# Weights of a fused attention and mixture-of-experts kernel loaded in pieces of 256 KB, with a new order of the first batch

## The chip, the cores and the metric

The kernel runs on one core of one Trainium2 chip. The metric is device time in microseconds (us), lower is better. TensorE is called PE here (its weight loads PEld), VectorE DVE, ScalarE ACT, GpSimd POOL, and SyncE, which issues every data transfer of this kernel, SP.

## The reference

There are two stages, in float32, over 8 batches, 8 heads, 576 positions and head width 64.

- Attention: `out = up(softmax(qd kd^T / 8) vd) + softmax(local(q k^T / 8)) v`. `qd`, `kd` and `vd` are means over groups of 4 positions, `up` repeats each row 4 times, and `local` keeps the positions less than 4 apart.
- The result, laid out as `x` of shape (8, 576, 512), goes through a mixture of 4 causal attention experts: `logits = x w_gate`; each expert has `q = x wq`, `k = x wk`, `v = x wv`, a causal softmax, and `(a v) wo`; for each position the two experts with the highest logits are summed, weighted by the softmax of those two logits.

## The kernel before

**Work and stages.** A batch `b` has four pairs of heads `c`. Stage 1 of a pair, written as (b, c), goes through these steps: `load` (q, k and two halves of v, with for batches from 1 on four smaller transfers of v for the pooling), `local` (scores of the band, L519, on PE), masking, maximum, exponential, sum and normalisation of them (`l_mask`, `l_max`, `l_sub`, `l_exp`, `l_sum`, `l_eps`, `l_rec`, `l_nrm`), `qd` and `kd` (means, L555 on DVE or L559 to L562 on POOL), `vd_mm` (the mean of v as a matmul, L577, in batch 0 alone), `down` (scores of the means, L594), their softmax (`d_max` to `d_nrm`), `tp` (transposes, L375, and their copies `tp_ev` out of PSUM to `pt` and `pd`, L317 or L319), `o1` and `o1d` (the matmuls with v, L656 to L668), `up`, `x`, and at last `xh` (ACT, L681), `xt` and `xl` (L684, L682), which split x into a high and a low part. Stage 2 makes the experts' `q`, `k` and `v` with three matmuls for each product (high by high, low by high, high by low; L709 and L770), and the gate. Stage 3 is the experts' causal attention (L858 to L977) and the output matmul.

**Weights.** `weights()` loads `wqk` (1 MB), `wvg` (520 KB) and `wo` (512 KB), each with one transfer into one staging tile `wst` (step `wld`). For each of the four chunks of 128 input rows (two for `wo`) ACT casts the high part (`whi`, L454), and POOL or DVE subtracts for the low part (`wlo`, L456). The staging tile of `wo` takes the place of that of `wqk`, so it waits until all chunks of `wqk` have been read.

**Order.** The program creates a list of steps, and `SEQ` says in which order they are emitted: a number divided by 4 is the step, the remainder chooses the engine where there is a choice (or which half of PSUM the `down` scores go to), and -1 is a filler matmul on zeros (L476), which also takes a PSUM buffer. Each engine works through its own queue in that order, and waits at the head of it. Four PSUM buffers `big0` to `big3` go round in the order in which they come free.

**Transfers.** Every transfer goes through `fetch` (L464) on SP's queue. From the 5th to the 60th transfer each waits for the landing of the one four places ahead, so at most four are under way (`PACE = 4, 60`). SP waits in order: what stands behind a waiting transfer waits too.

**From the start to the projections.** The first batch alone has no earlier batch beside it. PE's first projection matmul is that of `q` of batch 0; from it on PE has matmuls of several batches to choose from.

Of the kernel before, what the change touches and what calls it, by code (L numbers as in the profile page):

```python
# [277 lines left out]
def tile_attn_then_moe(ctx: ExitStack, tc: tile.TileContext, qT, kT, v, wqk, wvg, wo, out):  # L278
# [7 lines left out]
    D = 128 * NP  # L286
# [9 lines left out]
    op = plan.op  # L296

    def buf(pool, shape, name, bufs=2, dtype=F32, tag=None, fifo=True):
        b = Buf(pool, shape, dtype, name, tag or name, bufs)
        b.fifo = fifo  # L300
        return b
# [142 lines left out]
    def weights():  # L444
        for at, (src, n, m, whi, wlo) in zip(WAT, ((wqk, NP, 512, wqk_h, wqk_l), (wvg, NP, 260, wvg_h, wvg_l),
# [3 lines left out]
            st = buf(wk, [128, n, m], "wst", bufs, tag=tag)  # L449
# [678 lines left out]
```

## Time and profile before

| | |
|---|---|
| median of 3 runs | 457.27 us (454.79 to 457.93) |
| the profiled execution's own time | 455.93 us |
| its span in the trace | 454.2 us |
| instructions in the trace | 23423 |
| PE busy | 437.5 us (96% of the span) |
| DVE busy | 360.3 us (79%) |
| ACT busy | 342.9 us (76%) |
| POOL busy | 309.1 us (68%) |
| transfers, mean rate | 52.90 MB, 116 GB/s |

The span runs from the first to the last recorded instruction; the profiled execution's own time is 1.7 us more. The busy shares are averages over all stages. The page also cuts the span into 40 slices of 11.4 us, with each engine's busy share in each; the first four slices are the stage that the change touches.

### The profile page before, as it was taken

The numbers are of one execution on the slowest core, as the hardware profiler recorded it, in microseconds if no ns is written. First come the engines' busy times: TensorE is split into PE (matmuls) and PEld (weight loads), VectorE is DVE, ScalarE is ACT, GpSimd is POOL, SyncE is SP. The second block draws the span as 40 slices with busy tenths as digits, with TensorE's granted clock in tenths as the row PEclk, the third lists the DMA queues.
The fourth block names the chain that finished last, engine by engine and source line by source line (L and its number), as shares of the span: only waits on it lengthen the run. The fifth ranks groups of instructions, "written<-read, shape, count | busy, mean of one in ns | idle before, by whom it ended". The sixth has DMA issues, their size and how long they took to land.

```text
span 454.2 us, 23423 instructions
## 1 busy us (share of the span) xinstructions
PE 437.5 (96%) x9910; PEld 404.2 (89%) x9911; DVE 360.3 (79%) x1018; ACT 342.9 (76%) x1097; POOL 309.1 (68%) x507
## 2 busy tenths in 40 slices
PE   6787999999999999999999999999999999999996
PEld 4766999999998899998999998999999898999776
DVE  8778898888888699968978889678787977656862
ACT  7777689779877898776787787876797687547873
POOL 6766989996886987737886798849677464205240
PEclk9899999999999999999999999999999999999999
DMA  7665667532336552515332742256240130101022
GB/s 247 195 189 151 200 165 206 155 97 76 98 95 171 162 144 51 170 47 157 116 127 83 196 119 76 84 162 182 69 155 19 56 97 4 69 14 40 29 82 104
DMA packets 44312, 52.90 MB, mean 116 GB/s; under 512 B 4144, under 2 KB 27184, under 8 KB 44208
## 3 DMA queue, kind: packets, MB, share of 16 engines
q1 hardware_dynamic: 44208, 51.40, 38.3%
q8 instruction: 78, 1.28, 1.2%
q14 instruction: 26, 0.21, 0.1%
HBM read 40.90 MB, written 9.44 MB: 111 GB/s over the span
## 4 chain that ended last, share of the span: by engine, by line
PE 86%; DMA 7%; DVE 3%; ACT 1%; issue 1%; SPq 0%; POOL 0%; POOLq 0%
PE pj L709 23%; PE pv L709 11%; PE po L709 10%; PE sq L858 9%; PE o L968 7%; PE tq L375 5%; PE tp L375 4%; PE sc L519 4%; PE o L656 4%; PE scd L594 3%; DMA lq<-in_qT_dram 2%; DMA wst<-in_wqk_dram 2%; PE pv L770 2%; DMA lv<-in_v_dram 2%; PE o L663 2%; PE po L1007 1%
## 5 line engine op out<-in xcount | busy, mean ns | idle before, releaser
L881 ACT ACTIVATE pr<-pr,pst 128x384 f32<-128x384 f32 (+8 forms) x144 | 80.2, 559 | 18.3 <-DVE pst L878 17.3
L709 PE MATMUL pj<-xh,wqk_h 64*128 64x288 f32 x512 | 83.0, 306 | 0.0
L889 POOL TENSOR_SCALAR pr<-pr,pst,gt 128x512 f32<-128x512 f32 (+8 forms) x90 | 58.4, 657 | 31.5 <-DVE pst L886 30.0
L709 PE MATMUL pj<-xh,wqk_l 64*128 64x288 f32 x512 | 79.0, 291 | 0.0
L709 PE MATMUL pj<-xl,wqk_h 64*128 64x288 f32 x512 | 79.0, 291 | 0.0
L878 DVE CUSTOM_DVE_ANT_0 pr<-sq,causal_t 128x192 f32<-128x192 f32 (+8 forms) x144 | 64.5, 485 | 8.4 <-PE sq L858 7.8
L709 PEld LDWEIGHTS pj<-xh,wqk_h 64*128 64x128 f32 x512 | 51.7, 185 | 2.8 <-issue 1.7
L858 PE MATMUL sq<-k,q 64*64 64x64 f32 (+6 forms) x768 | 52.1, 371 | 0.0
L709 PEld LDWEIGHTS pj<-xh,wqk_l 64*128 64x128 f32 x512 | 51.6, 185 | 0.0
L709 PEld LDWEIGHTS pj<-xl,wqk_h 64*128 64x128 f32 x512 | 51.6, 184 | 0.0
L540 POOL TENSOR_TENSOR lp<-lp,lst 128x640 f32<-128x640 f32 x28 | 36.3, 1300 | 11.1 <-DVE lst L539 5.3
L858 PEld LDWEIGHTS sq<-k,q 64*64 64x64 f32 x768 | 32.2, 133 | 7.7 <-issue 0.3
L709 PE MATMUL pv<-wvg_h,xh 64*128 64x260 f32 x256 | 38.8, 292 | 0.0
L604 ACT ACTIVATE dp<-scd,dst 128x144 f32<-128x144 f32 x96 | 35.3, 376 | 4.3 <-PE sq L858 2.0
L709 PE MATMUL pv<-wvg_h,xl 64*128 64x260 f32 x256 | 37.1, 279 | 0.0
L709 PE MATMUL pv<-wvg_l,xh 64*128 64x260 f32 x256 | 37.1, 279 | 0.0
L317 ACT COPY ptb<-tq 128x384 f32<-128x384 f32 (+4 forms) x74 | 31.3, 481 | 7.2 <-PE tq L375 6.9
L709 PE MATMUL po<-oh,wo_h 64*128 64x288 f32 x224 | 35.2, 301 | 0.2
L709 PE MATMUL po<-ol,wo_h 64*128 64x288 f32 x224 | 34.5, 292 | 0.5 <-issue 0.5
L375 PE MATMUL tq<-ident,pr 64*128 64x64 f32 x736 | 33.8, 224 | 0.4 <-DVE oc L977 0.3
L709 PE MATMUL po<-oh,wo_l 64*128 64x288 f32 x224 | 34.2, 291 | 0.0
L968 PE MATMUL o<-ptb,vg 64*64 64x320 f32 (+2 forms) x512 | 31.7, 378 | 0.8 <-ACT ptb L317 0.5
(183 smaller groups left out, 1436.8 us busy)
## 6 DMA issues: line engine op xcount, KB each, us to landing
lv<-in_v_dram SPq DMA_DIRECT2D x64, 160.0 KB, 3.9
lk<-in_kT_dram SPq DMA_DIRECT2D x32, 292.0 KB, 3.9
lq<-in_qT_dram SPq DMA_DIRECT2D x32, 292.0 KB, 4.1
out_dram<-ot SPq DMA_DIRECT2D x28, 288.0 KB, 3.2
lr<-in_v_dram SPq DMA_DIRECT2D x19, 256.0 KB, 3.5
pool<-in_v_dram SPq DMA_DIRECT2D x9, 256.0 KB, 4.2
lr<-in_v_dram SPq DMA_DIRECT2D x38, 32.0 KB, 3.1
wst<-in_wqk_dram SPq DMA_DIRECT2D x1, 1024.0 KB, 8.8
```

The source lines that it names most:

```text
L317: A.copy(dst, src)
L375: T.transpose(ps()[:, 512 * x + z[x]:512 * x + z[x] + 64], data[r, 0:128], ident[r, r])
L519: T.matmul(sc()[halves[h ^ (t // 5)], 512 * (t // 5) + W * i:512 * (t // 5) + W * i + W], q()[r, z:z + 64], k()[r, z:z + W], start=True, s ...
L540: op("l_nrm", "GV", (pool_tt(n), dve(n)), lambda e: eng[e].tensor_tensor(p(), p(), st[:, :, 2:3].to_broadcast([128, NT, W]), op=OP.mult), ...
L604: A.activation(p()[:, t, :], scs()[:, at * t:at * t + SD], AF.Exp, bias=st[:, t, 4:5], scale=1.0 / 128.0, accum_out=st[:, t, 0:1])
L656: T.matmul(o()[r, 512 * x + z:512 * x + z + n], lv()[kr, t, r], pt()[kr, at, t, 0:n], start=True, stop=True)
L709: mine = T.matmul(self.out(z), self.w(c, i, z)[r], self.m(c, i, z)[r], start=phase == 0 and c == 0 and i == 0, stop=phase == 1 and c == se ...
L858: T.matmul(pss[x][0]()[halves[e ^ turned(t)], at_of[x] + at + to:at_of[x] + at + to + n1 - n0], q()[r, 64 * t:64 * t + 64], k()[r, n0:n1], ...
L878: op("s_max", "V", dve(n) + 4, lambda x=x, t=t, n=n, src=src: V.tensor_tensor_reduce(rows_of[t], src(), causal_t[:, S - 64:S + 256] if t = ...
L881: op("s_exp", "A", 281 + n / 1.2, lambda x=x, t=t, n=n: A.activation(rows_of[t], rows_of[t], AF.Exp, bias=st[:, x, 4:5], scale=-1.0, accum ...
L889: op("s_nrm", "GV", (327 + n / 1.2 + max(0, n - 384) * 1.1, 189 + n / 1.92), lambda g, x=x, t=t, n=n: eng[g].tensor_scalar(rows_of[t], row ...
L968: T.matmul(obs[x]()[r, q0:q1], vg()[kr, j, 64 * (2 * p + e):64 * (2 * p + e) + 64], pt()[kr, e, j, q0:q1], start=j == 0, stop=j == len(job ...
```

## The change

Each weight matrix is loaded in several transfers: `wqk` in four of one chunk (256 KB), `wvg` in two of two chunks (260 KB), `wo` in two of one chunk (256 KB), into the same staging tile. A chunk's cast waits for its own piece alone. That makes 5 more transfers, all through `fetch` with the same rule of four under way, so the 60th transfer comes five places earlier among the others.

The front of `SEQ` is written anew: its first 416 entries (of 2685) become 420 (of 2689). They hold the same steps, the five new transfers, and one filler matmul less. All entries behind them are the old ones with 20 added, since the five new steps shift the numbers. The new front reaches as far as the first two steps of the second half of `q` of batch 0.

```diff
@@ weights()
-            op("wld", "D", 1800 if m == 260 else 780 * n, lambda st=st, src=src: fetch(
-                st(), src.rearrange("(c p) j -> p c j", p=128)), w=[st], alloc=[st])
+            rows, step = src.rearrange("(c p) j -> p c j", p=128), 2 if m == 260 else 1
+            for c in range(0, n, step):
+                op("wld", "D", 900 if m == 260 else 780, lambda st=st, rows=rows, c=c, step=step: fetch(
+                    st()[:, c:c + step, :], rows[:, c:c + step, :]), w=[(st, c + x) for x in range(step)], alloc=[] if c else [st])
@@ SEQ (first entries; all behind entry 416 are the old ones plus 20)
-    4, 0, 177, 173, 120, 216, 136, 140, 188, 192, 268, 144, 16, -1, 197, 200, 124, 232, -1, 273, 220, 148, 236, 205,
...
```

What the new numbers mean, queue by queue:

| queue | before | after |
|---|---|---|
| SP, places 8 to 29 | k(0,3), k(1,0), q(0,3), q(1,0), v(0,1), v(0,2), v(0,1), k(1,1), q(1,2), v(0,2), **wqk**, v(0,3), v(0,3), q(1,1), **wvg**, k(1,2), k(1,3), q(1,3), then v of batch 1 | q(0,3), k(0,3), k(1,0), q(1,0), v(0,1) twice, **wqk 0**, v(0,2) twice, **wqk 1**, **wqk 2**, q(1,1), k(1,1), v(0,3) twice, k(1,2), **wvg 0**, q(1,2), **wqk 3**, **wvg 1**, k(1,3), q(1,3), then v of batch 1 |
| SP, `wo` | place 43 | place 35 (first piece) and place 49 (second) |
| SP, second half of v(1,1) | place 44 | place 47 |
| PE, ahead of the first `q` | 45 steps, 8 of them fillers | 43 steps, 6 of them fillers, the rest the same steps |
| PE, from `vd_mm`(0,0) on | vd_mm(0,0), tp(0,0), down(0,2), local(0,3), tp(0,0), o1(0,0), local(1,0), o1d(0,0), tp(0,1), vd_mm(0,1) | vd_mm(0,0), tp(0,0) twice, down(0,2), local(0,3), o1(0,0), o1d(0,0), local(1,0), tp(0,1), vd_mm(0,1) |
| PE, on to the first `q` | filler, down(0,3), tp(0,1), tp(0,2), vd_mm(0,2), o1(0,1), o1d(0,1), tp(0,2), filler, down(1,0), filler, o1(0,2), o1d(0,2), local(1,1), tp(0,3), vd_mm(0,3), 2 fillers, tp(0,3), filler, down(1,1), o1(0,3), o1d(0,3), local(1,2) | filler, tp(0,1), o1(0,1), tp(0,2) twice, o1d(0,1), down(0,3), down(1,0), filler, vd_mm(0,2), local(1,1), o1(0,2), o1d(0,2), vd_mm(0,3), tp(0,3) twice, 2 fillers, down(1,1), o1(0,3), o1d(0,3), local(1,2) |
| ACT, around the first cast of `wqk` | l_exp(0,3), xh(0,0), d_scl(0,3), tp_ev(0,1), d_exp(0,3), **whi 0**, vd_ev(0,2), l_exp(1,0), tp_ev(0,2) | l_exp(0,3), tp_ev(0,2) twice, **whi 0**, whi 2, l_exp(1,0) |
| moved from POOL to DVE, ahead of the first `q` | | qd(0,1), qd(0,2), qd(0,3), kd(0,3), wlo 2 of wqk, wlo 0, 2 and 3 of wvg |
| moved from DVE to POOL, ahead of the first `q` | | kd(0,1), kd(1,0), qd(1,0), xl and xt of (0,0), xl(0,2), wlo 3 of wqk |
| moved between ACT, POOL and DVE | d_nrm(0,0) on ACT, d_nrm(0,1) on POOL; copies of tp(0,1), vd_mm(0,3) on ACT, of tp(0,2), vd_mm(0,0) on DVE | d_nrm(0,0) on POOL, d_nrm(0,1) on ACT; the copies the other way round |

## Rows read from the trace of the kernel before

**Rows 1.** The page: busy time of each engine; PE's busy tenths in 40 slices.

```profile
PE 437.5 (96%) x9910; PEld 404.2 (89%) x9911; DVE 360.3 (79%) x1018; ACT 342.9 (76%) x1097; POOL 309.1 (68%) x507
...
PE   6787999999999999999999999999999999999996
```

**Rows 2.** Busy time by stretch (us, PE, PEld, DVE, ACT, POOL, clock, transfers).

```profile
0.00:42.09 42.09, 31.76 (x727) 25.19 (x729) 33.97 (x84) 31.90 (x106) 31.59 (x61) 0.96 0.68 197
...
45.00:400.00 355.00, 353.63 (x8280) 333.20 (x8281) 291.73 (x822) 274.32 (x885) 263.20 (x417) 1.00 0.40 116
```

**Rows 3.** Chain of work that ended last, 18 to 42 us (start, length, what).

```profile
18.75 8.79 DMA wst<-in_wqk_dram
...
27.56 0.62 ACT wqk_h L454
...
29.09 0.54 ACT pt L317
29.63 0.59 issue
...
33.51 0.46 PE tp L375 x10
...
34.83 0.65 issue
...
40.18 1.65 issue
```

**Rows 4.** Timeline of PE's weight loads: idle before and its end, in brackets.

```profile
22.05 1.08 PEld L577 LDWEIGHTS pv<-lv,pool 128*128 128x128 f32 x9 [1.25 <-issue]
...
30.22 0.10 PEld L476 LDWEIGHTS <-zero 128*128 128x128 bf16 x1 [1.50 <-issue]
...
35.48 0.63 PEld L577 LDWEIGHTS pv<-lv,pool 128*128 128x128 f32 x5 [0.84 <-issue]
...
41.83 0.19 PEld L519 LDWEIGHTS sc<-lk,lq 64*64 64x64 f32 x2 [1.78 <-issue]
```

**Rows 5.** Busy time by stretch, cut in the stops of Rows 4.

```profile
21.00:29.00 8.00, 6.66 (x126) 5.67 (x125) 6.77 (x15) 6.63 (x25) 5.35 (x7) 1.00 0.77 216
29.00:35.00 6.00, 4.46 (x126) 3.44 (x126) 4.53 (x14) 4.32 (x15) 4.43 (x6) 1.00 0.52 146
35.00:41.00 6.00, 4.65 (x126) 3.71 (x127) 5.80 (x15) 4.91 (x15) 6.00 (x7) 1.00 0.62 173
```

**Rows 6.** Transfer queues at 22.1:27.3 (all of them), 27.3:29 and 32.6:34.2 (packets, MB, share).

```profile
q1 hardware_dynamic: 1140, 1.33, 90.3%
...
q8 instruction: 1, 0.02, 5.0%
...
DMA  0009000000000000000000000000000000000000
...
q8 instruction: 1, 0.02, 5.1%
```

**Rows 7.** One tile: the fillers (ns, least, median, most).

```profile
L476 PE MATMUL wu<-zero x7: 379/389/390, 8.3 to 37.5; 128*128 128x512 bf16 x7
```

**Rows 8.** Groups by line, 4 to 42 us (busy, mean ns, idle before).

```profile
L682 POOL TENSOR_TENSOR xl<-x,xh 128x576 fp32r<-128x576 f32 x1 | 1.4, 1425 | 0.0
...
L682 DVE TENSOR_TENSOR xl<-x,xh 128x576 fp32r<-128x576 f32 x2 | 2.6, 1293 | 0.0
```

**Rows 9.** The page: transfers by line (KB each, median us to landing).

```profile
lr<-in_v_dram SPq DMA_DIRECT2D x19, 256.0 KB, 3.5
...
wst<-in_wqk_dram SPq DMA_DIRECT2D x1, 1024.0 KB, 8.8
```

**Rows 10.** Timelines: SP's places 26 and 44, and PE's first `o1` of (1,1).

```profile
36.63 0.60 SPq L464 DMA_DIRECT2D lv<-in_v_dram  x1
...
52.56 2.15 SPq L464 DMA_DIRECT2D lv<-in_v_dram  x1
...
61.55 0.30 PE L656 MATMUL o<-pt,lv 64*64 64x58 f32 x4
```

281 rows, old and new, of the table SEQ are left out of this document.

## The prediction, made before the changed kernel was run

> **What bounds the kernel now.** I read the page first. PE is busy for 96% of the span, and in the slices it is full from the fifth on; only the first four, 45 us, are at 6 to 8 tenths [rows 1]. Busy time by stretch says the same: before the first projection, which starts at 42.09, PE works 31.76 us of 42.09 and rests 10.33; from 45 to 400 it rests 1.4 us in 355 [rows 2]. Behind 45 us PE sets the pace and the order there is the old one, so what the new front can give is the time at which PE starts the projections, and it carries to the end one for one.
>
> Next the chain of waits, 18 to 42 us. It runs from the 1 MB transfer of `wqk` (18.75 to 27.54) to ACT's first cast of it at 27.56, over ACT's copy of `pt`, which ends at 29.63, to PE, and from there on it is PE itself with three stops called "issue": 0.59, 0.65, 1.65 [rows 3]. "issue" is time in which PE waits for nothing that the profile shows. The timeline of the weight loads has four such stops, ending at 22.05, 30.22, 35.48 and 41.83 [rows 4]. Counting by stretches cut in these stops shows what they are: 251, 252 and 253 matmuls and weight loads lie between one stop and the next (126 + 125, 126 + 126, 126 + 127) [rows 5]; with the few waits that PE's queue also holds, that is a block of the same number of instructions each time. The transfer queues show the other half: from 22.1 to 27.3 all packets are data, and the one packet of instructions runs in the stretch after it, in which the `wqk` transfer lands; and in 32.6 to 34.2, when the data has drained, a packet of instructions is all there is, at about 32.7 [rows 6], 2.7 us ahead of PE's restart at 35.48. So PE's instructions come in blocks, the block's packet waits behind data, and in this stage, full of short matmuls, PE gets to the end of a block before the next is there. Restart to restart takes 8.17, 5.26 and 6.35 us [rows 4]; PE's own work in those blocks is 6.66, 4.46 and 4.65 [rows 5].
>
> On this the Trainium skill ("Runtime: NRT & Kernel Launch", section Instruction fetch mechanics) says that instructions are fetched in blocks of 256 while the block before is worked on, and that crossing a boundary is mostly hidden. The count in the trace agrees with it; the stops do not. By the page the stops would have nothing to give and the result would be the second rival below.
>
> **The change, part by part.**
>
> Pieces of `wqk`. Before, the whole 1 MB had to land for ACT's first cast; the cast starts 0.02 after the landing, and it and two other steps stood ahead of the copy of `pt` [rows 3]. Now piece 0 is place 14 on SP instead of 18, it is a quarter of the size, and the cast stands behind both copies of tp(0,2). That takes ACT out of the second stop. It also takes a 1 MB transfer out of the way of the instruction packet, so I let the longest interval, 8.17, fall to what PE's work sets, 6.66 [rows 5], called 6.7; bounds 5.3 (the shortest interval) and 8.2 (nothing gained).
>
> Front of PE's queue. Ten more transposes (0.46 [rows 3]) now stand ahead of local(0,3), where PE works on the block before the first stop, so I put the first restart 0.5 later, at 22.5; bounds 0 and +0.8, the latter since qd(0,1) on DVE goes ahead of the first mask. The rest of that stretch is the same work in another order.
>
> Third and fourth block. They hold as many instructions as before. The third now has two of the mean matmuls of v in it, the fourth none, so PE's work moves from the fourth to the third, and I take the mean of the two measured intervals for each, (5.26 + 6.35) / 2 = 5.8 [rows 4]; bounds 5.3 and 6.4 each.
>
> Fillers. Two fewer stand ahead of the projections: 2 x 0.39 = 0.78 of PE work [rows 7]. It lies inside blocks that end with the refill, so 0; should the refills be quick, 0.78 is gained. One of them comes back later among busy matmuls and costs 0.39 there; I let that go into the bounds.
>
> Five more transfers. SP issues each in about 0.6 [rows 10], 3 us in all, in a stage in which it mostly waits for a slot: 0. Their landing: a transfer of 256 KB has a median of 3.5 us, the 1 MB took 8.8 [rows 9], so four in turn would be 14 and four abreast 3.5; the four pieces are spread over places 14 to 26, and chunk 3 is not needed before the fourth step of `q`, so 0, with bounds 0 and +1.
>
> Steps handed between engines. Seven means change sides, four to DVE and three to POOL; two xl go to POOL, where one takes 1.43 against 1.29 on DVE [rows 8]. Both engines are busy for 32 and 34 of the first 42 us [rows 2], so neither is full: 0. The last operand of the third step of `q`, xl(0,2), comes from POOL now; behind it there is room of some 2 us, and if that cover is gone it costs what it is late, bound +1.
>
> Sum: 22.5 + 6.7 + 5.8 + 5.8 = 40.8 for the fourth restart, and 0.26 as before from there to the first projection (41.83 to 42.09): 41.1 instead of 42.1, 1.0 us earlier. With the lower bounds 22.05 + 5.3 x 3 + 0.26 = 38.2, but the second block has 6.66 of work, so 39.5, 2.6 us earlier; with the upper ones 22.9 + 8.2 + 6.4 x 2 + 0.26 = 44.2, and 1 for the landing or for xl, which are waits of the same step, 3.1 us later. The sum is made against the profiled execution, 455.93, which gives 454.9. That execution was 1.3 under the median of the runs, 457.27; from the median it is **456.3**.
>
> **Rivals.**
>
> *No stops at all.* With small transfers the instruction packets could always be in time. Then PE needs only its work: 22.05 less the first stop of 1.25 is 20.8, and 6.66 + 4.46 + 4.65 + 0.26 make 36.8 [rows 4, 5], 5.3 earlier: 452.0. For it speaks that the packet waited behind the 1 MB. Against it: the stops at 35.48 and 41.83 came when that had long landed, with data of other transfers under way, which stay.
>
> *The change does nothing to the path.* The refills come when they came, the new order only changes which step stands at each stop: 457.3. For it: three of four stops had no part in `wqk`, and of the 1.50 of rest at the second, 0.59 is refill whatever ACT does [rows 3, 4]. Against it: the longest interval is the one with the 1 MB in it.
>
> *SP held by `wo`: slower.* The first piece of `wo` is place 35 instead of 43. It needs the staging tile, so SP stands until the last low part of `wqk` is made, now on POOL behind xl(0,2) and l_sub(1,1). Behind it wait 27 transfers of batches 1 and 2. Place 26 was issued at 36.63 and place 44 at 52.56, 0.89 each [rows 10]; the second half of v(1,1) is place 47 now, so 12 x 0.89 = 10.7 after SP is let go, and it lands 3.5 later [rows 9]. PE wanted it at 61.55 [rows 10], or 60.5 if it is 1.0 earlier. So it decides from 60.5 - 14.2 = 46.3 on, one for one: let go at 49, PE loses 2.7 and the time is 459.0. Against it: POOL's list puts that low part at about 42.
>
> The Trainium skill ("DMA: Bandwidth & Descriptors", section Bandwidth and the cost model before it) speaks against small transfers: some 2.0 us fixed for each, and 1 MiB or more in one. Five more would be 10 us in the queue, with four under way 2.5 us later, an estimate by that page; this rival would then be 461.5. Rows 9 agree in kind, 4 x 3.5 being more than 8.8.
>
> **How the numbers follow.** Forecast 456.3, chance 0.50, its own range 454.7 to 457.3 (2.6 earlier, or nothing); no effect 0.20; no stops 0.12; SP held, or the upper bounds, 0.18. The likeliest gives 456.3. A measurement of this kernel tells about 1%, 4.6 us, from no change, so the limits are 452.7 and 461.8. Faster by more than that needs nearly all stops to go: 0.11. Slower needs a hold past 52 us, or a loss behind 45 us that no row shows: 0.06. Within: 0.83. For 8 in 10 the range takes the forecast, no effect and SP held to 459.2, and on the lower side reaches from 454.7 towards the rival without stops, to 452.9.
>
> **What would show it.** Right: four stops of PE still a block apart, the second interval near 6.7 instead of 8.2, the first projection near 41, ACT's first cast without idle time before it, and from 45 us on a PE as full as before. Wrong: stops gone; intervals unchanged; PE idle in front of `o1` of (1,1) with a transfer as the releaser; or a difference that arises behind 67 us, where the order is the old one.

## The result, and the profile after

The changed kernel takes 449.80 us (median of 6 runs, 448.16 to 451.06); the kernel before, beside it, 454.97 (6 runs). The ratio is 0.988, 95% interval 0.983 to 0.992: 5.2 us or 1.2% faster. In a later series of runs it was 449.24 against 453.68, ratio 0.989 (0.984 to 0.993). The range of the prediction ended at 452.9, so the time lies outside it, next to the rival "no stops at all" (452.0). The profiled execution took 450.58, its span is 448.8.

The page after, for [rows 1]: PE works 1.7 us less in a span that is 5.4 us shorter, and is full from the third slice on instead of the fifth, but for the nineteenth (202 to 213 us).

```profile
PE 435.8 (97%) x9910; PEld 400.4 (89%) x9910; DVE 360.0 (80%) x1018; ACT 343.6 (77%) x1101; POOL 306.3 (68%) x507
...
PE   6899999999999999998999999999999999999996
```

Busy time by stretch, for [rows 2]: the first projection comes at 34.38 instead of 42.09; PE rests 5.9 us ahead of it instead of 10.3. From 45 to 400 us it rests 2.8 us instead of 1.4; 1.3 of that comes at 203 us (below).

```profile
0.00:34.38 34.38, 28.45 (x726) 22.26 (x726) 31.41 (x76) 29.16 (x96) 29.27 (x60) 1.00 0.77 227
45.00:400.00 355.00, 352.23 (x8191) 328.99 (x8191) 289.21 (x816) 273.33 (x878) 253.59 (x408) 1.00 0.39 113
```

The chain, for [rows 3]: no transfer of `wqk` in it, and from 19.22 on PE with no "issue" longer than 0.04 up to the first projection.

```profile
18.18 0.61 ACT pt L317
18.79 0.44 issue
19.22 1.72 PE pv L579 x14
...
24.95 1.83 PE pv L579 x14
...
30.27 0.99 PE tp L375 x20
...
34.45 1.40 PE pj L711 x17
```

Lines behind `weights()` have numbers 2 higher in this kernel. Of the four stops of [rows 4] one is left in the weight loads:

```profile
19.23 1.53 PEld L579 LDWEIGHTS pv<-lv,pool 128*128 128x128 f32 x13 [1.02 <-issue]
```

The stretches between the ends of the blocks (at 24.95, 30.30 and 34.38), for [rows 5]. Columns as in [rows 2]. With the waits that PE's queue holds, a block is 256 instructions, as before. PE works through all of the second stretch and nearly all of the third:

```profile
18.00:25.00 7.00, 5.81 (x131) 4.89 (x127) 6.32 (x15) 5.95 (x18) 6.07 (x9) 1.00 0.69 200
25.00:30.30 5.30, 5.30 (x126) 4.94 (x128) 5.10 (x13) 5.13 (x21) 4.74 (x5) 1.00 0.90 264
30.30:34.38 4.08, 3.92 (x131) 2.93 (x131) 3.87 (x12) 3.88 (x10) 4.08 (x5) 1.00 0.76 222
```

The transfer queues, for [rows 6], in 19.22:20.3 (data alone) and 20.3:21: the packet of instructions now starts 1.15 us behind PE's restart, where it was 5.4 before.

```profile
q1 hardware_dynamic: 134, 0.20, 54.9%
...
q8 instruction: 1, 0.02, 10.8%
```

A piece lands in 3.9 us, for [rows 9]; and SP issues the first piece of `wo` at 36.96, so it is not held, and the second half of v(1,1) at 48.36 instead of 52.56, for [rows 10].

```profile
wst<-in_wqk_dram SPq DMA_DIRECT2D x4, 256.0 KB, 3.9
```

```profile
36.96 0.55 SPq L466 DMA_DIRECT2D wst<-in_wo_dram  x1
...
48.36 0.60 SPq L466 DMA_DIRECT2D lv<-in_v_dram  x1
```

### The profile page after: what moved, and what is told of

Read it like the earlier page. It is cut to its first block, busy times and chain, and to the rows that moved or that the text cites. A ratio compares the mean times of both kernels' runs of the same rounds, so it can differ in the third digit from the quotient of the medians.

```text
span 448.8 us, 23428 instructions
## 1 busy us (share of the span) xinstructions
PE 435.8 (97%) x9910; PEld 400.4 (89%) x9910; DVE 360.0 (80%) x1018; ACT 343.6 (77%) x1101; POOL 306.3 (68%) x507
## 3 DMA queue, kind: packets, MB, share of 16 engines
q8 instruction: 78, 1.28, 1.3%
## 4 chain that ended last, share of the span: by engine, by line
PE 88%; DMA 3%; DVE 3%; ACT 3%; issue 1%; POOL 1%; SPq 1%; DVEq 0%; POOLq 0%
PE pj L711 22%; PE pv L711 10%; PE po L711 9%; PE sq L860 9%; PE o L970 8%; PE tq L375 5%; PE tp L375 4%; PE o L658 4%; PE sc L521 4%; PE scd L596 3%; PE o L665 2%; DMA lr<-in_v_dram 2%; PE pv L772 2%; PE po L1009 1%; PE pv L579 1%; PE o L974 1%
## 5 line engine op out<-in xcount | busy, mean ns | idle before, releaser
L711 PE MATMUL pj<-xh,wqk_h 64*128 64x288 f32 x512 | 81.6, 306 | 0.0
L711 PE MATMUL pj<-xl,wqk_h 64*128 64x288 f32 x512 | 78.1, 291 | 0.0
L711 PEld LDWEIGHTS pj<-xh,wqk_h 64*128 64x128 f32 x512 | 50.5, 185 | 2.0 <-issue 1.0
L711 PEld LDWEIGHTS pj<-xh,wqk_l 64*128 64x128 f32 x512 | 50.4, 185 | 0.8 <-issue 0.8
L711 PEld LDWEIGHTS pj<-xl,wqk_h 64*128 64x128 f32 x512 | 50.4, 184 | 0.2 <-issue 0.2
L711 PE MATMUL po<-oh,wo_l 64*128 64x288 f32 x224 | 34.2, 291 | 0.0
L375 PEld LDWEIGHTS tq<-ident,pr 64*128 64x128 f32 x736 | 30.0, 138 | 3.8 <-issue 2.3
```

Of the source, the lines that this page charges most:

```text
L375: T.transpose(ps()[:, 512 * x + z[x]:512 * x + z[x] + 64], data[r, 0:128], ident[r, r])
L711: mine = T.matmul(self.out(z), self.w(c, i, z)[r], self.m(c, i, z)[r], start=phase == 0 and c == 0 and i == 0, stop=phase == 1 and c == se ...
```

## The experiments

In all of them "stop" is a rest of PE at the end of a block, and "packet" the start of PE's packet of instructions, found by narrowing the stretch in the view of the queues. "Behind" counts from PE's restart at the end of the second block, unless a crossing (PE's passing from one block into the next) is named. The expectations count blocks from the kernel's start: there the second block ends near 19 us (22 where its stop is long), and the third to fifth are those that the prediction calls the second to fourth.

**Either half alone.** The pieces with the old order, and the new order with whole matrices.

```diff
 split_only: weights() and pieces of the kernel after; SEQ of the kernel before,
+            the extra pieces right behind the first of their matrix
 order_only: weights() of the kernel before; SEQ of the kernel after,
-            without the extra pieces
```

> The order of the kernel before, with the three weight matrices in pieces of 256 KB; the extra pieces stand right behind the first piece of their matrix on SP, everything else is in its old place. Theory T (transfers): PE's instruction packets wait behind data in the transfer engines, and smaller pieces let them through. Then the four refill stops, 4.84 us in sum before, fall to about 1.5 us, the packet at 27.4 comes near 24, the first projection comes near 38.5 instead of 42.1, and the time is about 3 us (0.7%) below before. Theory O (order): the gain comes from the new order of the first batch. Then the stops stay between 4 and 5 us in sum, the first projection stays at 41 to 42, and the time is within 0.2% of before.

> The new order of the first batch, with each weight matrix in one transfer again, at the place of its first piece. Theory T: the first operand of the v mean still lands about 1 us earlier, and PE works there at full clock, together 2.3 us; but the refill stops come back (3 us or more in sum) where wqk is under way, so the first projection comes near 38.5 to 40 and the time is 2 to 3 us below before. Theory O: the first projection comes at 34.5 to 35 as in the kernel after, with at most one stop, and the time is within 0.2% of the kernel after (5 us below before).

Neither half gives anything by itself: 453.52, ratio 0.999 (0.996 to 1.001), and 454.34, ratio 1.003 (1.000 to 1.006). The weight loads of the first show three stops (that at the end of the third block is gone):

```profile
19.31 1.42 PEld L586 LDWEIGHTS pv<-lv,pool 128*128 128x128 f32 x12 [1.15 <-issue]
...
32.13 0.97 PEld L586 LDWEIGHTS pv<-lv,pool 128*128 128x128 f32 x8 [1.66 <-issue]
...
38.59 0.19 PEld L528 LDWEIGHTS sc<-lk,lq 64*64 64x64 f32 x2 [1.89 <-issue]
```

and those of the second a single one, three times as long:

```profile
21.89 2.85 PEld L584 LDWEIGHTS pv<-lv,pool 128*128 128x128 f32 x13 [3.34 <-issue]
```

Its packet starts at 19.28, 4.0 us behind PE's crossing into the block before (15.32), with the 1 MB under way; with pieces it was 1.05 (15.20 to 16.24), and 0.7 to 2.7 in the five profiles with that front. Behind that stop the granted clock falls, which is one more loss, and eleven of the twelve runs have a mean clock of 0.988 to 0.996 as the profiled one has (0.996), so the long stop is hardly that execution's alone. The same kernel's PE by stretch (busy, clock, transfers):

```profile
20.00:25.00 5.00, 3.11 (x15) 0.66 0.76 185
```

Neither theory was right. The order takes away the stops at the ends of the third to fifth block, but with the 1 MB whole the one at the end of the second grows to 3.45. The pieces shorten that one in the new order; in the old order they do not (1.07, against 1.17 and 0.66 in two profiles with whole matrices). It needs both.

**Depth of the transfers.**

```diff
-PACE = 4, 60
+PACE = 8, 60        (after_pace8; before_pace2 has 2 in the kernel before)
```

> The kernel after, with eight transfers under way at a time instead of four in the first sixty. Theory T: packets wait behind twice as much data; they start 2 to 4 us past the block's boundary instead of 0.9 to 1.3, two or three stops of 0.6 to 1.5 us come back, and the first projection moves from 34.4 to 36 or 37. Theory O: the depth of the data queue is nothing to PE; the first projection stays within 0.5 us of 34.4, or comes earlier because loads land earlier.

> The kernel before, with two transfers under way at a time instead of four in the first sixty. Theory T: where the queue holds less data the packets come sooner, so the stops at 35.5 and 41.8 shrink below 0.3 us each, while the one behind the 1 MB of wqk stays; PE waits longer for loads instead, so the time can go either way. Theory O: the stops stay at their four places with 4 to 5 us in sum, and later loads only add waits: first projection later than 42.1 and the time above before.

With eight under way the packets start 3.9 us behind the crossing at 14.96 and 4.1 behind the restart at 21.79; one stop of 3.71 comes of it, the first projection is at 38.53, and the time 452.01, ratio 0.996 (0.993 to 0.999). So the packet came later with more data under way, though there was one long stop, not the two or three expected. With two under way PE waits for loads (2.81 and 4.13 us and more), 479.25, ratio 1.056; a packet came 7.2 us behind its crossing even there, and three stops stayed (1.91, 0.29 and 0.55), so that run did not tell the theories apart.

**The same kernels once more.**

> The kernel before, unchanged, profiled once more, to see what in its first 42 us is the kernel's and what is that one execution's. Theory C (a chain of late blocks: a block of PE instructions that comes late is followed by late ones until PE has long work): four stops at the same four places again, 4 to 5.5 us in sum, packets 2.3 to 5.4 us behind the crossings, PE going on 2.4 to 2.9 us behind each packet. The late landing at 12.81 and the low clock behind it are that execution's: here the first v mean starts near 11 at full clock, and the first projection comes near 40. Rival: landing and clock are the kernel's as well, and the first projection comes at 42 again.

> The kernel after, unchanged, profiled once more. Theory C: the stop at the end of the second block is about 1 us at most, no other stop ahead of the first projection, which comes at 34 to 35; the losses at 203 us (1.4) and 260 us (0.7) are that execution's and are not there again, or stand elsewhere. Rival: they belong to the kernel, since everything is earlier by 7 us there, and come again within 1 us of the same places.

The kernel before (453.63) has its first v mean at 10.39 and its first projection at 38.06, 4.0 us earlier than in the execution on which the prediction was built. The four stops are there again (3.81 us in PE's idle time, 4.84 in the first profile):

```profile
18.54 1.42 PEld L577 LDWEIGHTS pv<-lv,pool 128*128 128x128 f32 x12 [0.74 <-issue]
...
26.16 0.10 PEld L476 LDWEIGHTS <-zero 128*128 128x128 bf16 x1 [0.95 <-issue]
31.45 0.97 PEld L577 LDWEIGHTS pv<-lv,pool 128*128 128x128 f32 x8 [0.80 <-issue]
37.80 0.19 PEld L519 LDWEIGHTS sc<-lk,lq 64*64 64x64 f32 x2 [1.78 <-issue]
```

with PE's own work in the three blocks as in [rows 5], and a low clock behind the last stop, which costs 1.4 us: the 127 matmuls of 37.80:45.00 take 7.20, and as many take 5.77 behind the same stop in the first profile (41.83:47.60), where the clock is 1.00:

```profile
18.00:26.00 8.00, 6.66 (x126) 5.67 (x125) 7.28 (x15) 5.89 (x23) 4.89 (x7) 1.00 0.89 240
26.00:31.40 5.40, 4.45 (x126) 3.45 (x126) 4.41 (x13) 5.34 (x17) 5.40 (x6) 1.00 0.66 194
31.40:37.80 6.40, 4.65 (x127) 3.71 (x128) 6.13 (x15) 5.26 (x18) 6.40 (x8) 1.00 0.54 151
37.80:45.00 7.20, 7.20 (x127) 6.71 (x128) 4.57 (x7) 2.76 (x6) 3.48 (x6) 0.76 0.71 192
```

The kernel after (446.81) has one stop of 0.33, its first projection at 33.51, and lost nothing at 203 or 260 us. So the two losses were not in every execution; that at 203 us came again in a third profile (below).

**Which matrix, and three under way.**

```diff
 wqk_pieces: weights(), new SEQ without the second pieces of wvg and wo
-  rows, step = ..., 2 if m == 260 else 1
+  rows, step = ..., 1 if (n, m) == (NP, 512) and whi is wqk_h else n
 after_pace3: PACE = 3, 60 in the kernel after
```

> The new order, with wqk alone in pieces; wvg and wo go in one transfer each, at the place of their first piece. Theory C: what decides is that the packet for the third block, requested at about 15 us, gets past wqk; so the stop there stays near 1 us, no other one follows, the first projection stays at 34 to 35.5, and the time is within 0.3% of the kernel after, 1% below before. Rival (any transfer over 256 KB holds a packet up): wvg, 520 KB at about 25 us, delays the packet behind 24.95, a stop of 1 us or more comes at 30.3, and half of the gain is gone.

> The kernel after, with three transfers under way at a time instead of four in the first sixty. Theory C: less data ahead of the packets, so no refill stop is left; but two transfers under way already gave a kernel whose PE waits for loads, so waits for q, k and v of 0.5 to 2 us each come in their place, and the time is 0 to 2% above the kernel after. Rival (the data is what holds PE up in the whole stage): without any stop the first projection comes at 33.5 or earlier, and the time falls by another 0.2%.

`wqk` alone in pieces gives the whole gain: 449.57, ratio 0.985 (0.979 to 0.991), first projection 34.50, one stop of 0.95; the 520 KB of `wvg` did no harm. With three under way PE rests 0.56 at the end of the second block, where a load of v comes last, but it waits 1.92 and 2.12 us for k and q of batch 1: 454.82, ratio 1.003 (0.999 to 1.006).

**Whose order.** The new front could be split between SP and the four other engines (not between PE and the other three, whose orders hang together).

```diff
 sp_new: weights() in pieces; SP's steps in the order of after, all other engines' as before
 sp_old: weights() in pieces; SP's steps in the old order, all other engines' as after
```

> The loads on SP in the new order, with pieces; PE, DVE, ACT and POOL in the old order (SP's list of the kernel after, everything else from the one before). Theory S: what lies in the transfer engines when PE asks for a block decides, so SP's order is the half of the new order that counts: packets 0.4 to 2 us behind the crossings, no stops at the ends of the third to fifth block, the first projection at 35 to 36, and the time 4 us (0.9%) below before. Theory P: PE's own order decides (where its long and its short work lies between the crossings): packets 2.3 us or more behind the crossings, two or three stops of 0.6 to 1.7 us as in the split kernel with the old order, the first projection at 38 to 39, and the time within 0.4% of before.

> The reverse: the loads on SP in the old order, the extra pieces right behind the first of their matrix, and PE, DVE, ACT and POOL in the new order. Theory S: stops of 0.6 to 1.7 us at the ends of the third to fifth block, the first projection at 38 to 39, the time within 0.4% of before. Theory P: after the end of the second block no stop, packets 0.4 to 2 us behind the crossings, the first projection at 34 to 36, and the time 3 to 5 us below before; a wait for a load that the new order wants earlier could cost up to 1 us of it.

SP's new order alone: 454.84, ratio 0.999 (0.996 to 1.002). Its profile is better than that, with two stops and the first projection at 36.59:

```profile
18.62 1.42 PEld L586 LDWEIGHTS pv<-lv,pool 128*128 128x128 f32 x12 [0.60 <-issue]
...
36.33 0.19 PEld L528 LDWEIGHTS sc<-lk,lq 64*64 64x64 f32 x2 [0.90 <-issue]
```

but it was one of four runs at 451.2 to 452.3, all with a mean clock of 1.00; the other eight took 454.4 to 455.4, seven of them at 0.989 to 0.996. The other engines' new order with the old loads: 451.42, ratio 0.992 (0.989 to 0.995), with one stop and none behind it, although PE waited 1.82 us for a k at 6 us in its profile, whose execution, 454.44, was slower than all its others but one:

```profile
21.16 2.83 PEld L586 LDWEIGHTS pv<-lv,pool 128*128 128x128 f32 x13 [1.60 <-issue]
```

So theory P holds for the larger part. And the packet goes with PE's order, not with what SP has under way: 3.4 us behind in sp_new, 1.1 in sp_old. The expectation "2.3 or more" in sp_new was right there and two blocks on (4.2), and wrong in between (1.2).

**Where the block begins, or what lies in it.**

```diff
-WAT, NW0 = (53.0, 30.0, 67.0), 7
+WAT, NW0 = (53.0, 30.0, 67.0), 8     (split_nw8, on split_only; after_nw6 has 6 in the kernel after)
```

> The old order with pieces, and one more matmul of zeros ahead of everything (eight instead of seven), which moves every block boundary of PE two instructions back in the work: the third block then begins with the first instruction of a group of v means, as in the new order, instead of inside it. Theory P1 (where the boundary falls in PE's stream decides how soon the next packet comes): the packet behind that boundary starts 1.1 to 1.6 us behind PE's restart instead of 3.4 to 5.4, one or two of the later stops go, and the first projection comes at 35.5 to 37.5. Theory P2 (what work lies between the boundaries decides): packets 3 us or more behind, stops at the ends of the fourth and fifth block again, the first projection at 38 to 39, the time as that of the split kernel with the old order.

> The kernel after with one matmul of zeros less ahead of everything (six instead of seven), which moves every block boundary two instructions on: the third block begins inside the group of v means, as in the old order. Theory P1: the packet behind that boundary starts 3 us or more behind the restart, stops of 0.6 us or more come at the ends of the third to fifth block, the first projection moves to 36.5 to 38, and half of the gain is gone. Theory P2: the packet starts 1.1 to 1.6 us behind the restart, there is no stop behind the second block, and the first projection stays at 33.5 to 36.5 and the time within 0.3% of the kernel after.

P2 holds on both sides. In the old order the packet is 5.0 us behind and PE rests at the same four block ends (0.78, 0.54, 1.31 and 1.48; the first of them ends with ACT's copy of `pt`, 3.4 us behind its packet), first projection 38.59, 452.91, ratio 0.997 (0.993 to 1.000). In the new order it is 1.9 behind, there is no stop at all, first projection 33.55, 448.31, ratio 0.988 (0.982 to 0.994), which can't be told from the kernel after.

**The loss at 203 us, and a faster version.**

```diff
 SP, from place 145:  load of pool for (4,2), half of v (4,2),
+  both loads of lr for (4,3),
   load of pool for (5,1) (held until 194 us), lr for (5,0), half of v (4,3),
-  both loads of lr for (4,3),
```

> The kernel after, with the two loads of lr for (4,3) moved on SP from place 150 to right behind place 146, ahead of the transfer for which SP is held until 194; they are issued near 190 instead of 196. In three of five profiles with the new order the landing of this lr at about 199.7 lets POOL start its 1.9 us xl ahead of DVE's vd, which then takes 1.54 instead of 0.53, and PE loses 1.3. If this is what gives back part of the gain, DVE waits for nothing there, vd takes 0.53 in the profile, PE has no idle time at 200 to 205, and the median falls by 0.5 to 1 us below that of the kernel after (to about 1.3% below before). Rival: DVE waits there for something else as well or PE has the slack, and the time stays within 0.2% of the kernel after.

> The kernel after, unchanged, timed next to the same kernel with lr earlier, since the two were only compared over different calls. The median lies at 448.5 to 450, the ratio to before at 0.986 to 0.990; in its profile the first projection at 33.5 to 36.5 by the stop at the end of the second block (0.3 to 2.3 us).

> The kernel after with the two loads of lr for (4,3) earlier on SP, unchanged, next to the kernel after. If DVE's wait for that lr costs PE 1.3 us in three of five executions, the median is 0.5 to 1 us below that of the kernel after of this call. Rival: the difference seen before was one of chips and calls, and the two medians lie within 0.4 us.

447.82, ratio 0.985 (0.982 to 0.989); and beside the kernel after in one series 447.31 against 449.24 (ratios to before 0.985 (0.980 to 0.989) and 0.989 (0.984 to 0.993)): 1.9 us, more than the 0.5 to 1 expected; the fastest version here. In the third profile of the kernel after DVE waits for `lr`, POOL starts `xl` ahead of DVE's `vd`, and PE loses 1.13. DVE, POOL and PE there:

```profile
201.19 0.74 DVE L573 TENSOR_TENSOR lr<-lr 128x512 f32<-128x512 f32 x1 [1.25 <-DMA lr<-in_v_dram]
201.97 1.53 DVE L574 TENSOR_TENSOR vd<-lr 128x256 f32<-128x256 f32 x1
...
201.35 1.87 POOL L684 TENSOR_TENSOR xl<-x,xh 128x576 fp32r<-128x576 f32 x1
...
204.94 0.40 PE L375 MATMUL tq<-ident,pr 64*128 64x64 f32 x6 [1.13 <-DVE pd L319]
```

With `lr` earlier (second profile) there is no wait, `vd` runs ahead of `xl`, and PE has no idle time at 200 to 205:

```profile
198.25 0.67 DVE L580 TENSOR_TENSOR lr<-lr 128x512 f32<-128x512 f32 x1
198.96 0.48 DVE L581 TENSOR_TENSOR vd<-lr 128x256 f32<-128x256 f32 x1
...
200.42 1.43 POOL L691 TENSOR_TENSOR xl<-x,xh 128x576 fp32r<-128x576 f32 x1
```

Two of three profiles of the kernel after have this loss, neither of the two with `lr` earlier. What gives the rest of the 1.9 us was not looked for.

Up to some 190 us the kernel with `lr` earlier is the kernel after, so its two profiles are two more of the new front. The first of them has the longest stop of the five, and its first projection at 36.35; its time, 450.49, and that of one more run, 450.13, lie above the other four (447.27 to 447.86). PE there, its stop and the stretch around the restart (busy, clock, transfers):

```profile
21.19 1.72 PE L586 MATMUL pv<-lv,pool 128*128 128x128 f32 x14 [2.29 <-ACT lp L539]
...
20.00:25.00 5.00, 3.81 (x85) 1.00 0.75 212
```

The packet starts at 18.52, 2.7 us behind the crossing at 15.83, with pieces and four transfers under way; PE goes on 2.7 behind it. So the length of the first stop differs from one execution to the next even in the changed kernel.

## Why the prediction was wrong, step by step

PE's idle time at block ends ahead of the first projection, its start, and the packet behind the restart, from the profiles:

| kernel | stops, us | first projection | packet behind |
|---|---|---|---|
| before; once more | 4.84; 3.81 | 42.09; 38.06 | 5.4; 4.8 |
| before, two under way | 2.75 | 48.58 | 7.2 (crossing) |
| old order, pieces | 4.29 | 38.84 | 3.8 |
| old order, pieces, blocks moved | 4.11 | 38.59 | 5.0 |
| SP new, others old, pieces | 1.28 | 36.59 | 3.4 |
| SP old, others new, pieces | 1.71 | 37.94 | 1.1 |
| new order, whole matrices | 3.45 | 38.47 | 2.0 |
| after, eight under way | 3.71 | 38.53 | 4.1 |
| after, three profiles | 1.13; 0.33; 1.18 | 34.38; 33.51; 34.63 | 1.2; 1.6; 2.5 |
| after, `lr` earlier, two profiles | 2.29; 0.35 | 36.35; 33.62 | 1.1; 2.1 |
| after, `wqk` alone in pieces | 0.95 | 34.50 | 1.1 |
| after, three under way | 0.56 | 35.88 | 1.1 |
| after, blocks moved | 0 | 33.55 | 1.9 |

**What was right.** PE sets the pace behind 45 us and a gain at the first projection reaches the end; the stops are block ends (256 instructions apart, 251 to 254 of them matmuls and weight loads and the rest waits of PE's queue; where nothing else comes last, PE goes on 2.2 to 3.0 us behind a packet). The five transfers and the handed steps, put at 0, cost nothing: from 19.22 to the first projection PE waits for no transfer and no other engine. SP was let go at 36.96, ahead of the 46.3 from which the rival with `wo` would have decided. The first restart was to come 0.5 later: 18.54 in the repeated kernel before, 18.35, 18.46, 18.89, 19.22 and 21.19 in the five profiles of the new front, a median of 0.35 later.

**The step that failed** is "third and fourth block": it let the stops stay, at the mean of the measured intervals, 5.8 each, with bounds 5.3 and 6.4. After the change (in the prediction's count) the third takes 5.36 and the fourth 4.07 (24.95, 30.31, 34.38), which is PE's own work in them; the second takes 5.73 where 6.7 was put, since the new order has other work in it. Together 15.2 instead of 18.3. The stop at the end of the fourth was back once, with 0.52 in the third profile. The two fillers, put at 0 "should the refills be quick, 0.78", then counted.

**The argument that misled** was "the stops at 35.48 and 41.83 came when that had long landed, with data of other transfers under way, which stay". It is true that they don't hang on `wqk`: the new order with whole matrices has none there either. But they don't hang on that data: they go with the order of PE and the three engines beside it, which the prediction treated as "the same work in another order". That every packet waits behind data does not hold in the kernel before itself. Between PE's restart at 35.48 and the packet at 39.13 the transfer engines stood empty for 1.1 us; their busy tenths in 35.5:39, 40 slices:

```profile
DMA  9952000000000000000699593955789877879999
```

The repeated profile shows the same (empty from 31.96 to 33.20, packet at 35.04). The 0.12 for "no stops at all" was far too low, and the range stopped short of it.

**The base** was an execution with 4.0 us of its own ahead of the first projection: the v mean waited for v until 12.81, and the granted clock was 0.79 in 10:15 and 0.87 in 15:20 (1.00 in both after). In 20 of 29 runs of the kernel before in one series, and 10 of 23 in another, the mean clock was 0.999 or more, so that part is not in every execution. The median of three runs that the forecast started from, 457.27, was also 2.3 above that of the six (454.97), so of the 6.5 us between 456.3 and 449.80 some 2.3 are the base and 4.2 the gain, 5.2 instead of 1.0. The base did not spoil the sum, which was a difference, but the rival's 36.8 came from it; by the repeated profile it would have been 17.8 + 6.66 + 4.45 + 4.65 + 0.26 = 33.8, and 33.5 to 36.4 was measured. That the rival's 5.3 earlier is so near to the 5.2 measured is in part luck: the stop at the end of the second block did not go in most profiles, and the low clock of some executions of the kernel before is in the 5.2. In the sum, 22.05 + 6.66 + 5.3 x 2 + 0.26 is 39.6 and not 39.5, which changes nothing.

**Where the time is.** Between the two repeated profiles the first projection moves 4.55 us: 3.48 of stops, 0.78 of fillers, 0.3 of the rest. The low clock behind the last stop, 1.4, goes too. That is 6.0 of the 6.9 us between their spans (451.9 and 445.0). The first profile after kept 3.1 of it, mainly since its first projection was 0.9 later and it lost 1.3 at 203 us and 0.7 at 260.

The Trainium skill ("Runtime: NRT & Kernel Launch", section Instruction fetch mechanics) says that crossing a block is mostly hidden. From 45 us on the trace agrees, with 1.4 us of rest in 355; in the new order it agrees in part, with 0.3 to 2.3 us in 34 to 36; in the old order it does not, with 3.8 to 4.8 us in 38 to 42.

**Open.** Why the packet comes 1.1 to 2.5 us behind the restart in the new order and 3.4 to 5.4 in the old one. It is not the place at which a block begins, as far as a shift by two instructions tells, and not the order of SP's transfers; with more data under way it was longer (4.1 with eight), but the engines that stood empty ahead of the packet at 39.13 show that data is not all of it. Nor is it known why the packet behind the crossing at 15 us comes 0.7 us later in one execution and 2.7 in another. Which of the moved steps does it was not found. Later stops at block ends (0.1 to 0.7 us, at other places in each profile) were not studied.

## What to carry to other kernels

Look at what a stage's short instructions ask of the instruction supply: rests called "issue" at a constant count of instructions are a cost of their own, and they vanish or come back with an order of work that looks equivalent. When two halves of a change each give nothing, they can still give 1.2% together, as here, where one half took later stops away and made the first longer, and the other half shortened that. And profile a kernel twice before taking its first tens of us apart: 4 of 42 us were one execution's, and the first projection of the new front came at 33.5 to 36.4 in five profiles.

## What the runs showed of the hardware that was not expected

- Where PE stood at a block's end and nothing else came last, it went on 2.2 to 3.0 us behind the start of its packet of instructions; the packet came later with more data under way (0.5 us behind the crossing at 15 us with three transfers, 0.7 to 2.7 in five profiles with four, 3.9 with eight or with a 1 MB one; one profile each but for the four).
- A rest of PE of 3.45 us was followed by a granted clock of 0.66 in 20:25 (order_only), one of 1.65 by 0.76 in 37.8:45 (the kernel before, repeated). The length of the rest does not decide alone: behind the same 1.65 in the first profile of the kernel before, and behind 2.29 in the first one with `lr` earlier, the clock is 1.00.
- DVE's `vd` takes 0.48 or 1.53 us by whether POOL's `xl` has started before it. The Trainium skill ("SBUF — State Buffer", section SBUF: two separate sides) calls the port pair that the two engines share an exclusive lock for a whole instruction; the trace agrees in kind, since `vd` ends at 203.50, behind the end of `xl` at 203.22. In the repeated profile of the kernel after DVE waited 0.71 for this `lr` instead of 1.05 or 1.25, `vd` took 0.53, and PE lost nothing.
